# Reordering the first chunk of an attention + max-out kernel: separate softmax for two head pairs, their v parts between weight matmuls, and half of a set of sums moved from POOL to VectorE

## Chip, cores and metric

The kernel runs on one core of a Trainium2 chip. The metric is the device time of one execution in microseconds (us); lower is better. The times quoted are medians of several executions unless said otherwise. Each execution also reports a *span* (first to last instruction) and the *mean granted clock* of TensorE, where 1.0 is full speed. *Throttle* here means a stretch in which that clock is below 1.0, and no more: the profile shows the clock, not what sets it.

In the profile, PE is TensorE (PEld its weight loads), ACT ScalarE, DVE VectorE, POOL GpSimd. `L522` is a source line of the kernel profiled; the change moves line numbers, so the same helper is L522 before and L460 after.

## The reference

```python
k_proj = einsum('ks,bhsd->bhkd', E, k)          # sequence 1024 projected to 64
v_proj = einsum('ks,bhsd->bhkd', F, v)
attn   = softmax(q @ k_proj.T / 8)              # 8 batches, 8 heads, head dim 64
x      = (attn @ v_proj), heads side by side    # 8192 tokens x 512
h      = maximum(maximum(x @ w1, x @ w2), x @ w3)   # 512 -> 768
out    = h @ w_out                              # 768 -> 512
```

## The kernel before

Heads are worked on in four pairs (g = 0 to 3). A pair's output fills one 128-row slice of x, so slice `ct` of the weight matmuls needs only pair `ct`. For one pair, a *k part* or *v part* is the projection of k or v (with E or F), the *score product* is q times projected k, the *value product* is the softmax's exponentials times projected v, and the *scaling* divides that by the exponentials' sum. The token chunk is 512 wide. The order of instructions on each engine is that of the program (`manual_schedule`), and the matmuls' results go to one PSUM tile that the kernel declares as eight banks of 128x512 fp32 and deals out by its own helpers (`bank`, `two`).

The first chunk of the first batch is special. Nothing is loaded yet, so it is arranged around the loads: two pairs are finished first, then matmuls with slices 0 and 1 of w1 and w2 fill TensorE while the other two pairs are prepared. The parts that matter here, with cuts marked:

```python
C0 = (0, SPC)
...                                   # E, F transposed; q and k of pairs 0 and 1
z01 = []
for g in range(2):                    # pairs 0 and 1
    idle(2)                           # matmuls on zeros, to keep TensorE busy
    z01.append(sums(0, g, *C0))
    invert(0, g, *C0, z01[g])         # 1/sum as exp(-ln(sum)) on ACT
    v_pair(g)                         # v projected, copied by DVE
idle(1)
for g in range(2):
    scale_x(0, g, *C0, values(0, g, *C0))
...
def up_first(work):
    ...
    h = six()                         # six banks: w1, slices 0 and 1
    ...                               # copied to s1 (SBUF) by ACT and DVE
    then(0)                           # pairs 2 and 3: q, k, scores, one exp, one sum
    h = six()                         # six banks: w2
    for ct in range(2):
        for jt in jts:
            up_mm(h[jt][0], 1, 0, 0, jt, (ct,))
    then(2)                           # v 2, x 2, v 3, x 3, one after another
    for jt in jts:
        t, ns = bank()
        up_mm(t, 0, 0, 0, jt, (2, 3), first=2)            # w1, slices 2 and 3
        copy("s", s2[:, jt], t, ns)                       # ACT
        nc.gpsimd.tensor_tensor(out=s1[:, jt], in0=s1[:, jt], in1=s2[:, jt], op=ALU.add)
        added = clock["s"] + 1.2
        up_mm(h[jt][0], 1, 0, 0, jt, (2, 3))              # w2, slices 2 and 3
        most(s1[:, jt], *h[jt], s1[:, jt], added)         # DVE maximum
    then(4)
    for jt in jts:                                        # w3, all slices
        t, ns = bank()
        up_mm(t, 2, 0, 0, jt, range(NCT))
        most(hTs[0, 0][:, jt, :], t, ns, s1[:, jt])
        then(5 + jt)                  # second half of the queries, in between
...
up_first({
    0: [lambda: q_duo(1), lambda: k_pair(2), lambda: k_pair(3),
        lambda: attend(1), lambda: idle(3), lambda: sum_duo(1)],
    2: [lambda: v_pair(2), lambda: x_pairs(1, (0,)),
        lambda: v_pair(3), lambda: x_pairs(1, (1,))],
    5: [qp(0, (0, 1), *c1)],          # q transposes of the second half
    6: [qp(0, (2, 3), *c1)],
    7: [sc(0, 0, *c1)],               # its first score product
    8: [sc(0, 1, *c1)],
    10: [za(0, 0, *c1), sc(0, 2, *c1)],
})
```

I call the loop with w1's slices 2 and 3 the *last phase* of w1 and w2, and the score product under key 7 *the first score product of the second half*. That product is a good mile mark: after it both kernels do the same work in the same order.

The softmax here doesn't subtract the row's maximum and nothing guards it: scores larger than these inputs give would overflow.

Of the kernel before, what the change touches and what calls it, by code (L numbers as in the profile page):

```python
# [8 lines left out]
FP32 = mybir.dt.float32  # L9
BF16 = mybir.dt.bfloat16  # L10
AF = mybir.ActivationFunctionType
ALU = mybir.AluOpType
# [3 lines left out]
def kernel(  # L16
# [13 lines left out]
    nc = tc.nc  # L30
# [7 lines left out]
    P = 128  # L38
    HALF = 64
# [34 lines left out]
    def two():  # L74
        n = min(range(0, 8, 2), key=lambda n: max(free[n:n + 2]))
        deal((n, n + 1))
        return psum_t[:, n:n + 2, :], (n, n + 1)
# [6 lines left out]
    def pe(dt, wait=0.0):  # L84
        clock["pe"] = max(clock["pe"], wait) + dt
        return clock["pe"]

    def runs(eng, ready, dt, ns=()):
        if eng in clock:
            clock[eng] = max(clock[eng], ready + 0.06) + dt  # L90
            for n in ns:
                free[n] = clock[eng]
            return clock[eng]
        return ready + dt
# [139 lines left out]
    def sums(b, g, lo, nsi):  # L234
        return pair_mm(b, g, lo, nsi, lambda rows, hp: ones[rows])

    def invert(b, g, lo, nsi, z):
        t, ns, ready = z
        zl = att.tile([P, 2, CHUNK], FP32, name="zl", bufs=1)[:, :, 0:nsi * HALF]
        nc.scalar.activation(out=zl, in_=t, func=AF.Ln)  # L240
        runs("s", ready, 0.17 + nsi * 0.107, ns)
        if nsi == SI:
            zi = att.tile([P, 2, CHUNK], FP32, name="zi", bufs=2)
        else:
            zi = att.tile([P, 2, CHUNK // 2], FP32, name="zi0", bufs=4)
        nc.scalar.activation(out=zi, in_=zl, func=AF.Exp, scale=-1.0)  # L246
        zis[b, g, lo] = zi, runs("s", ready, 0.17 + nsi * 0.107)
# [129 lines left out]
    def idle(n):  # L377

        t, ns = bank()
        for _ in range(n):  # L380
            nc.tensor.matmul(out=t, lhsT=warm[:, 0:P], rhs=warm, start=True, stop=True)  # L381
        free[ns[0]] = pe(n * MM)
# [45 lines left out]
            t.rearrange("a (g si p) -> a g si p", si=SPC, p=P), ns, 0.7,  # L428
        )

    N0 = SPC * HALF

    def sc_duo(u):
        t, ns = two()
        for gg in range(2):
            g = 2 * u + gg
            for c in range(2):
                for hp in range(2):
                    rows = slice(hp * HALF, (hp + 1) * HALF)
                    at = g * SI + c * SPC // 2  # L440
                    nc.tensor.matmul(
                        out=t[c * HALF:(c + 1) * HALF, hp, gg * N0:(gg + 1) * N0],
                        lhsT=kpTs[0][rows, g, :],
                        rhs=qTs[0][rows, at:at + SPC // 2, :],
                        start=True, stop=True,
                    )
        return t, ns, pe(0.5)

    def exp_duo(u, sc):
        t, ns, ready = sc  # L450
        pTs[0, u] = att.tile([P, 2, CHUNK], BF16, name="pT", bufs=4)
        nc.scalar.activation(out=pTs[0, u], in_=t, func=AF.Exp, scale=scale)
        runs("s", ready, 1.0, ns)

    def sum_duo(u):
        t, ns = two()
        for c in range(2):
            rows = slice(c * HALF, (c + 1) * HALF)
            for hp in range(2):
                nc.tensor.matmul(  # L460
                    out=t[hp * HALF:(hp + 1) * HALF, c],
                    lhsT=ones[rows], rhs=pTs[0, u][rows, hp, :],
                    start=True, stop=True,
                )
        ready = pe(0.25)
        zl = att.tile([P, 2, CHUNK], FP32, name="zl", bufs=1)
        nc.scalar.activation(out=zl, in_=t, func=AF.Ln)
        runs("s", ready, 1.0, ns)
        zi = att.tile([P, 2, CHUNK], FP32, name="zi", bufs=2)
        nc.scalar.activation(out=zi, in_=zl, func=AF.Exp, scale=-1.0)  # L470
        zis[0, u] = zi, runs("s", ready, 1.0)

    def x_pairs(u, pairs):

        t, ns = two()
        for i, gg in enumerate(pairs):
            for c in range(2):
                rows = slice(c * HALF, (c + 1) * HALF)
                for hp in range(2):
                    nc.tensor.matmul(  # L480
                        out=t[hp * HALF:(hp + 1) * HALF, c, i * N0:(i + 1) * N0],
                        lhsT=vps[0][rows, 2 * (2 * u + gg) + hp, :],
                        rhs=pTs[0, u][rows, hp, gg * N0:(gg + 1) * N0],
                        start=True, stop=True,
                    )
        ready = pe(0.15 * len(pairs))
        zi, when = zis[0, u]
        for i, gg in enumerate(pairs):
            g = 2 * u + gg
            nc.vector.tensor_tensor(  # L490
                out=xTs[0][:, g, 0:SPC, :].rearrange("a (c s) p -> a c (s p)", c=2),
                in0=t[:, :, i * N0:(i + 1) * N0],
                in1=zi[:, :, gg * N0:(gg + 1) * N0],
                op=ALU.mult,
            )
            runs("v", max(ready, when), 0.69, ns)

    C0 = (0, SPC)
    idle(11)
    turn_ef()  # L500
# [3 lines left out]
    k_pair(1)  # L504
    for g in range(2):
        exps(0, g, *C0, scores(0, g, *C0))
    z01 = []
    for g in range(2):
        idle(2)
        z01.append(sums(0, g, *C0))  # L510
        invert(0, g, *C0, z01[g])
        v_pair(g)
    idle(1)
    for g in range(2):
        scale_x(0, g, *C0, values(0, g, *C0))

    ffn_sb = ctx.enter_context(tc.tile_pool(name="ffn_sb", bufs=2))
    hTs = {}
# [16 lines left out]
    def up_first(work):  # L535


        def then(key):
            run_later()
            for f in work.get(key, []):  # L540
                f()

        s1 = ffn_sb.tile([P, NJT, CHUNK], FP32, name="s1", bufs=1)
        s2 = ffn_sb.tile([P, NJT, CHUNK], FP32, name="s2", bufs=1)
        hTs[0, 0] = ffn_sb.tile([P, NJT, CHUNK], BF16, name="hT")
        jts = range(NJT)

        def six():
            return [(t[:, n], ns[n:n + 1]) for t, ns in (two(), two(), two()) for n in (0, 1)]

        h = six()
        for ct in range(2):
            for jt in jts:
                up_mm(h[jt][0], 0, 0, 0, jt, (ct,), last=1)
                if ct == 1:
                    copy("sv"[jt % 2], s1[:, jt], *h[jt])
        then(0)
        load_k1()
        h = six()
        for ct in range(2):  # L560
            for jt in jts:
                up_mm(h[jt][0], 1, 0, 0, jt, (ct,))
        then(2)
        for jt in jts:
            t, ns = bank()
            up_mm(t, 0, 0, 0, jt, (2, 3), first=2)
            copy("s", s2[:, jt], t, ns)
            nc.gpsimd.tensor_tensor(out=s1[:, jt], in0=s1[:, jt], in1=s2[:, jt], op=ALU.add)
            added = clock["s"] + 1.2
            up_mm(h[jt][0], 1, 0, 0, jt, (2, 3))  # L570
            most(s1[:, jt], *h[jt], s1[:, jt], added)
        then(4)
        for jt in jts:
            t, ns = bank()
            up_mm(t, 2, 0, 0, jt, range(NCT))
            most(hTs[0, 0][:, jt, :], t, ns, s1[:, jt])
            then(5 + jt)
# [132 lines left out]
    for b in range(B):  # L710
        p = plan(b)

        def behind(ch, step):
            for f in p.get((ch, step), []):
                f()

        for ch in range(NCHUNK):
            if (b, ch) == (0, 0):
                c1 = (SPC, SPC)
                def attend(u):  # L720
                    exp_duo(u, sc_duo(u))

                up_first({
                    0: [lambda: q_duo(1), lambda: k_pair(2), lambda: k_pair(3),
                        lambda: attend(1), lambda: idle(3), lambda: sum_duo(1)],
                    2: [lambda: v_pair(2), lambda: x_pairs(1, (0,)),
                        lambda: v_pair(3), lambda: x_pairs(1, (1,))],
                    5: [qp(0, (0, 1), *c1)],
                    6: [qp(0, (2, 3), *c1)],
                    7: [sc(0, 0, *c1)],  # L730
                    8: [sc(0, 1, *c1)],
                    10: [za(0, 0, *c1), sc(0, 2, *c1)],
                })
                run_later()
                behind(0, NJT - 1)
            else:
                for step in range(NJT):
                    up(b, ch, step)
                    behind(ch, step)
            for tt in range(SPC):  # L740
                down(b, ch, tt, "v" if (b, ch) == (0, 0) else "s")
                behind(ch, NJT + tt)
# [30 lines left out]
```

## Time and profile before

| | before |
|---|---|
| time, median of 3 runs | 411.93 us (411.62 to 412.19) |
| span of the profiled execution | 409.9 us |
| PE busy | 394.5 us, 96% |
| DVE, ACT, POOL busy | 200.9, 194.1, 38.6 us |

PE is the bound, so only TensorE's waits, and time at a lower clock, can be won without removing work. The first view is two lines of the page of the kernel before: busy time by engine, and the granted clock in 40 slices of the span (each digit a tenth, 9 is 90% or more; a slice is 10.2 us).

```profile
PE 394.5 (96%) x2452; PEld 180.5 (44%) x2497; DVE 200.9 (49%) x308; ACT 194.1 (47%) x281; POOL 38.6 (9%) x49
...
PEclk9989999999999999999999999999999999999999
```

The third slice of the granted clock is 8: something happens between 20.5 and 30.7 us. The next view is the timeline of that stretch of the kernel before. Its columns are start, duration, engine, source line, operation, output<-input, how many instructions were merged, and in brackets the idle time just ahead with what ended it.

```profile
9.17 0.70 PE L406 MATMUL banks<-efT,k_t 128*64 128x64 bf16 x32
...
21.17 2.76 PE L522 MATMUL banks<-xT,w_sb 128*128 128x512 bf16 x12
...
23.86 0.64 PE L288 MATMUL banks<-v_t,efT 128*64 128x128 bf16 x16
...
24.96 0.30 PE L480 MATMUL banks<-pT,vp 64*64 64x256 bf16 x4 [0.46 <-DVE vp L99]
...
26.13 0.64 PE L288 MATMUL banks<-v_t,efT 128*64 128x128 bf16 x16 [0.87 <-DVE xT L490]
...
27.15 0.30 PE L480 MATMUL banks<-pT,vp 64*64 64x256 bf16 x4 [0.38 <-DVE vp L99]
...
28.25 0.58 PE L522 MATMUL banks<-xT,w_sb 128*128 128x512 bf16 x1 [0.80 <-DVE xT L490]
...
31.67 6.18 POOL L568 TENSOR_TENSOR s<-s,s 128x512 f32<-128x512 f32 x5 [0.45 <-ACT s L99]
...
37.89 0.69 DVE L532 TENSOR_TENSOR s<-banks,s 128x512 f32<-128x512 f32 x1 [0.54 <-PE banks L299]
...
39.09 0.68 DVE L99 COPY qT<-banks 128x1024 bf16<-128x1024 bf16 x1
...
39.83 0.30 PE L207 MATMUL banks<-qT,kpT 64*64 64x256 bf16 x4 [1.00 <-DVE qT L99]
```

Twelve w2 matmuls run to 23.93. Then come v part, copy, value product and scaling (DVE, L490) of pair 2, and the same again for pair 3. The w2 sums hold six of the eight banks, and the two left are handed from one step to the next, so the steps are in series: TensorE works 1.9 us of 4.3. The last phase starts at 28.25. Below it, POOL makes the six w1 additions one after another (6.18 us for five of them); the last maximum on DVE (37.89) waits for the last of these (the view names PE's q transposes, which ended at the same moment, but the earlier maxima name POOL, and so does this one in the profile of e5 below), hence the q copy at 39.09, and TensorE idles 1.00 us until the first score product of the second half at 39.83.

The windows view of the same profile gives busy time of each engine in a stretch (PE, PEld, DVE, ACT, POOL, with the number of instructions in brackets), after it the granted clock (0.75 in the first row), and last two columns on DMA:

```profile
27.00:28.00 1.00, 0.30 (x4) 0.21 (x5) 0.59 (x2) 0.00 (x0) 0.00 (x0) 0.75 1.19 217
28.00:29.00 1.00, 0.58 (x1) 0.25 (x2) 0.20 (x1) 0.00 (x0) 0.00 (x0) 0.50 1.20 192
29.00:30.00 1.00, 0.94 (x3) 0.38 (x3) 0.00 (x0) 0.58 (x1) 0.04 (x1) 0.50 1.44 200
30.00:31.00 1.00, 1.00 (x4) 0.35 (x3) 0.00 (x0) 0.00 (x0) 1.00 (x1) 0.54 1.45 199
```

The clock is 1.00 before and after these four rows. It is halved from the middle of the first until just before 31: (1-0.75)/0.5 + 1 + 1 + (1-0.54)/0.5 = 3.4 us. (In windows of 0.25 us it reads 1.00 in 27.25:27.50, 0.52 in 27.50:27.75, 0.50 until 30.75 and 0.66 in 30.75:31.00.)

### The profile page before, as it was taken

What the parts mean: (1) busy time and instruction counts of PE and PEld (TensorE: products, weight loads), DVE (VectorE), ACT (ScalarE), POOL (GpSimd) and SP (SyncE); (2) the same over time, 40 slices, a digit from 0 to 9 for tenths busy, and PEclk for the clock granted to TensorE, in tenths of its full rate; (3) what the DMA queues carried; (4) which work ended last, traced back from release to release, by engine and by line L of the source; (5) the groups of instructions that cost most, each with busy time, mean ns of one, the idle gap of its engine ahead of it and who ended that gap; (6) DMA issues with size and microseconds to landing.
All of it is one profiled execution on the core that took longest, in us unless ns stands there. A gap on an engine that the chain in (4) does not pass through costs nothing.

```text
span 409.9 us, 6124 instructions
## 1 busy us (share of the span) xinstructions
PE 394.5 (96%) x2452; PEld 180.5 (44%) x2497; DVE 200.9 (49%) x308; ACT 194.1 (47%) x281; POOL 38.6 (9%) x49
## 2 busy tenths in 40 slices
PE   8878999999999999999999999999999999999995
PEld 3434454345444544444544445444544444444443
DVE  2416656464374536636463564525465363525251
ACT  2523627722765266457435555536545556432322
POOL 7328002002000200200020002000000000000000
PEclk9989999999999999999999999999999999999999
DMA  9999937958934994794799109960420202020202
GB/s 169 204 206 196 190 117 112 222 159 125 243 65 114 211 224 139 128 233 83 117 209 224 69 2 244 204 168 0 105 104 1 102 2 102 2 102 0 104 0 103
DMA packets 58492, 52.30 MB, mean 128 GB/s; under 512 B 25952, under 2 KB 54112, under 8 KB 58464
## 3 DMA queue, kind: packets, MB, share of 16 engines
q0 software_dynamic: 28496, 28.31, 43.6%
q1 hardware_dynamic: 29824, 23.46, 18.0%
q8 instruction: 19, 0.31, 0.3%
q10 hardware_dynamic: 144, 0.13, 0.1%
q14 instruction: 9, 0.07, 0.1%
HBM read 57.15 MB, written 16.78 MB: 180 GB/s over the span
## 4 chain that ended last, share of the span: by engine, by line
PE 91%; DVE 3%; ACT 2%; DMA 2%; issue 1%; SPq 0%; DVEq 0%; ACTq 0%
PE banks L522 60%; PE banks L632 19%; PE banks L227 4%; PE banks L288 4%; PE banks L207 2%; DMA ef_f<-in_F_dram 1%; PE banks L299 1%; PE banks L381 1%; DMA out_dram<-o_sb 0%; DVE xT L257 0%; DVE s L99 0%; ACT zl L240 0%; ACT pT L218 0%; DVE xT L490 0%; DVE m L597 0%
## 5 line engine op out<-in xcount | busy, mean ns | idle before, releaser
L522 PE MATMUL banks<-xT,w_sb 128*128 128x512 bf16 x1117 | 255.5, 380 | 3.7 <-DVE xT L490 0.8
L522 PEld LDWEIGHTS <-w_sb 128*128 128x128 bf16 x1152 | 110.0, 98 | 139.5 <-issue 13.5
L597 DVE TENSOR_TENSOR m<-banks,h1s 128x512 f32<-128x512 f32 x90 | 62.1, 690 | 86.3 <-ACT h1s L593 54.7
L593 ACT COPY h1s<-banks 128x512 f32<-128x512 f32 x90 | 52.4, 582 | 92.9 <-PE banks L522 89.7
L632 PE MATMUL banks<-wout_sb,hT 128*128 128x512 bf16 x370 | 84.8, 379 | 0.8 <-issue 0.3
L257 DVE TENSOR_TENSOR xT<-banks,zi 128x1024 bf16<-128x1024 f32 (+1 forms) x34 | 38.3, 1130 | 75.3 <-ACT zi L246 57.7
L532 DVE TENSOR_TENSOR hT<-banks,m 128x512 bf16<-128x512 f32 x90 | 62.3, 692 | 9.7 <-PE banks L522 0.5
L99 ACT COPY o_sb<-banks 128x512 f32<-128x512 f32 (+1 forms) x60 | 34.8, 580 | 53.1 <-PE banks L632 53.0
L632 PEld LDWEIGHTS <-hT 128*128 128x128 bf16 x378 | 36.0, 98 | 45.5 <-issue 3.1
L240 ACT ACTIVATE zl<-banks 128x1024 f32<-128x1024 f32 (+1 forms) x34 | 32.3, 949 | 30.5 <-PE banks L227 30.2
L218 ACT ACTIVATE pT<-banks 128x1024 bf16<-128x1024 f32 (+1 forms) x34 | 32.1, 951 | 7.6 <-PE banks L207 7.6
L246 ACT ACTIVATE zi<-zl 128x1024 f32<-128x1024 f32 (+1 forms) x34 | 33.4, 981 | 1.1
L196 POOL DMA_DIRECT2D q_t<-in_q_dram x7 | 6.2, 882 | 193.9 <-DMA qT<-q_p 70.9
L288 PEld LDWEIGHTS <-efT 128*64 128x64 bf16 x288 | 13.7, 110 | 4.4 <-issue 4.0
L227 PE MATMUL banks<-pT,ones 64*64 64x512 bf16 (+1 forms) x136 | 13.3, 381 | 0.8 <-DVE xT L257 0.3
L207 PE MATMUL banks<-qT,kpT 64*64 64x512 bf16 (+1 forms) x136 | 12.7, 364 | 1.4 <-DVE qT L99 1.0
L99 DVE CAST vp<-banks 64x256 bf16<-64x256 f32 (+1 forms) x18 | 7.1, 397 | 12.5 <-PE banks L288 8.9
L227 PE MATMUL banks<-pT,vp 64*64 64x512 bf16 (+1 forms) x136 | 12.6, 359 | 0.0
L288 PE MATMUL banks<-v_t,efT 128*64 128x256 bf16 (+1 forms) x176 | 9.9, 254 | 0.9 <-DVE xT L490 0.9
L227 PEld LDWEIGHTS <-ones 64*64 64x64 bf16 x136 | 4.0, 103 | 14.9 <-issue 14.9
L99 ACT COPY s<-banks 128x512 f32<-128x512 f32 x9 | 5.1, 588 | 10.5 <-remote 5.9
L381 PE MATMUL banks<-warm 128*128 128x512 bf16 x23 | 8.3, 501 | 1.5 <-DVE warm L165 1.2
(56 smaller groups left out, 118.8 us busy)
## 6 DMA issues: line engine op xcount, KB each, us to landing
out_dram<-o_sb SPq DMA_DIRECT2D x30, 512.0 KB, 3.4
k_t<-in_k_dram POOLq DMA_DIRECT2D x7, 1024.0 KB, 14.1
q_t<-in_q_dram POOLq DMA_DIRECT2D x7, 1024.0 KB, 9.6
v_t<-in_v_dram POOLq DMA_DIRECT2D x7, 1024.0 KB, 18.5
w_sb<-in_moe_w_dram POOLq DMA_DIRECT2D x6, 384.0 KB, 14.4
k_t<-in_k_dram POOLq DMA_DIRECT2D x2, 512.0 KB, 9.4
v_t<-in_v_dram POOLq DMA_DIRECT2D x4, 256.0 KB, 10.7
wout_sb<-in_moe_w_out_dram POOLq DMA_DIRECT2D x1, 768.0 KB, 16.3
```

The costliest lines, as they stand in the source:

```text
L99: done = {"v": nc.vector.tensor_copy, "s": nc.scalar.copy, "g": nc.gpsimd.tensor_copy}[eng](out=o, in_=i)
L218: nc.scalar.activation(out=pTs[b, g, lo], in_=t, func=AF.Exp, scale=scale)
L227: nc.tensor.matmul(out=t[hp * HALF:(hp + 1) * HALF, c, 0:nsi * HALF], lhsT=w(rows, hp), rhs=p[rows, hp, :], start=True, stop=True,)
L240: nc.scalar.activation(out=zl, in_=t, func=AF.Ln)
L246: nc.scalar.activation(out=zi, in_=zl, func=AF.Exp, scale=-1.0)
L257: nc.vector.tensor_tensor(out=xTs[b][:, g, lo:lo + nsi, :].rearrange("a (c s) p -> a c (s p)", c=2), in0=t, in1=zi, op=ALU.mult,)
L288: nc.tensor.matmul(out=t[hh * HALF:(hh + 1) * HALF, 0:width], lhsT=efT[:, si, kv - 1, :], rhs=qkv[b][kv][:, heads[hh], si, :], start=(si = ...
L522: nc.tensor.matmul(out=h, lhsT=w_sb[i][:, ct, jt * P:(jt + 1) * P], rhs=xTs[b][:, ct, ch * SPC:(ch + 1) * SPC, :], start=(ct == first), st ...
L532: nc.vector.tensor_tensor(out=o, in0=h, in1=other, op=ALU.max)
L593: nc.scalar.copy(out=h1s, in_=h[0][0])
L597: nc.vector.tensor_tensor(out=m12, in0=h[1][0], in1=h1s, op=ALU.max)
L632: nc.tensor.matmul(out=o_ps, lhsT=hTs[b, ch][:, jt, tt * P:(tt + 1) * P], rhs=wout_sb[:, jt, :], start=(jt == 0), stop=(jt == NJT - 1),)
```

## The change

The intent: let pair 2 be ready earlier by giving pairs 2 and 3 each their own softmax instead of one shared; put their v parts between w2 matmuls so that TensorE does not stand still while DVE copies and scales; use slice 2 of w2, which needs only pair 2, to cover pair 3; relieve POOL of every second w1 sum. The start is reordered in the same way (pair 0's x before pair 1's v part).

```diff
-    z01 = []
-    for g in range(2):
-        idle(2)
-        z01.append(sums(0, g, *C0))
-        invert(0, g, *C0, z01[g])
-        v_pair(g)
     idle(1)
-    for g in range(2):
-        scale_x(0, g, *C0, values(0, g, *C0))
+    z(0); v_pair(0); z(1)                 # z: sums and their inverse
+    idle(1)
+    x(0); v_pair(1); x(1)                 # x: value product and scaling
 ...
         for ct in range(2):
             for jt in jts:
                 up_mm(h[jt][0], 1, 0, 0, jt, (ct,))
-        then(2)
+            then(1 + ct)
+        for jt in jts:
+            up_mm(h[jt][0], 1, 0, 0, jt, (2,))
+            if jt == 2:
+                then(3)
         for jt in jts:
             t, ns = bank()
             up_mm(t, 0, 0, 0, jt, (2, 3), first=2)
-            copy("s", s2[:, jt], t, ns)
-            nc.gpsimd.tensor_tensor(out=s1[:, jt], in0=s1[:, jt], in1=s2[:, jt], op=ALU.add)
-            ...
+            if jt % 2:
+                copy("s", s2[:, jt], t, ns)
+                nc.gpsimd.tensor_tensor(... op=ALU.add)
+            else:
+                nc.vector.tensor_tensor(out=s1[:, jt], in0=t, in1=s1[:, jt], op=ALU.add)
+            up_mm(h[jt][0], 1, 0, 0, jt, (3,))
+            ...                           # maxima: even jt at once, odd jt two steps later
 ...
-    0: [q_duo(1), k_pair(2), k_pair(3), attend(1), idle(3), sum_duo(1)],
-    2: [v_pair(2), x_pairs(1, (0,)), v_pair(3), x_pairs(1, (1,))],
+    0: [attend],     # q_duo(1), k_pair(2), k_pair(3); exps(2), exps(3); idle(2); z(2), z(3)
+    1: [v_pair(2)],
+    2: [x(2), v_pair(3)],
+    3: [x(3)],
```

(Semicolons and the comments in the diff are mine, to shorten it.)

More of the change, by code (lines that the diff above doesn't have):

```diff
@@ L429, in q_duo @@
         )
-    N0 = SPC * HALF
-    def sc_duo(u):
-        t, ns = two()
-        for gg in range(2):
-            g = 2 * u + gg
-            for c in range(2):
-                for hp in range(2):
-                    rows = slice(hp * HALF, (hp + 1) * HALF)
-                    at = g * SI + c * SPC // 2
-                    nc.tensor.matmul(
-                        out=t[c * HALF:(c + 1) * HALF, hp, gg * N0:(gg + 1) * N0],
-                        lhsT=kpTs[0][rows, g, :],
-                        rhs=qTs[0][rows, at:at + SPC // 2, :],
-                        start=True, stop=True,
-                    )
-        return t, ns, pe(0.5)
@@ L449, in exp_duo @@
-    def exp_duo(u, sc):
-        t, ns, ready = sc
-        pTs[0, u] = att.tile([P, 2, CHUNK], BF16, name="pT", bufs=4)
-        nc.scalar.activation(out=pTs[0, u], in_=t, func=AF.Exp, scale=scale)
-        runs("s", ready, 1.0, ns)
-    def sum_duo(u):
-        t, ns = two()
-        for c in range(2):
-            rows = slice(c * HALF, (c + 1) * HALF)
-            for hp in range(2):
-                nc.tensor.matmul(
-                    out=t[hp * HALF:(hp + 1) * HALF, c],
-                    lhsT=ones[rows], rhs=pTs[0, u][rows, hp, :],
-                    start=True, stop=True,
-                )
-        ready = pe(0.25)
-        zl = att.tile([P, 2, CHUNK], FP32, name="zl", bufs=1)
-        nc.scalar.activation(out=zl, in_=t, func=AF.Ln)
-        runs("s", ready, 1.0, ns)
-        zi = att.tile([P, 2, CHUNK], FP32, name="zi", bufs=2)
-        nc.scalar.activation(out=zi, in_=zl, func=AF.Exp, scale=-1.0)
-        zis[0, u] = zi, runs("s", ready, 1.0)
@@ L473, in x_pairs @@
-    def x_pairs(u, pairs):
-        t, ns = two()
-        for i, gg in enumerate(pairs):
-            for c in range(2):
-                rows = slice(c * HALF, (c + 1) * HALF)
-                for hp in range(2):
-                    nc.tensor.matmul(
-                        out=t[hp * HALF:(hp + 1) * HALF, c, i * N0:(i + 1) * N0],
-                        lhsT=vps[0][rows, 2 * (2 * u + gg) + hp, :],
-                        rhs=pTs[0, u][rows, hp, gg * N0:(gg + 1) * N0],
-                        start=True, stop=True,
-                    )
-        ready = pe(0.15 * len(pairs))
-        zi, when = zis[0, u]
-        for i, gg in enumerate(pairs):
-            g = 2 * u + gg
-            nc.vector.tensor_tensor(
-                out=xTs[0][:, g, 0:SPC, :].rearrange("a (c s) p -> a c (s p)", c=2),
-                in0=t[:, :, i * N0:(i + 1) * N0],
-                in1=zi[:, :, gg * N0:(gg + 1) * N0],
-                op=ALU.mult,
-            )
-            runs("v", max(ready, when), 0.69, ns)
@@ L506, with z, x @@
         exps(0, g, *C0, scores(0, g, *C0))
-    z01 = []
-    for g in range(2):
-        idle(2)
-        z01.append(sums(0, g, *C0))
-        invert(0, g, *C0, z01[g])
-        v_pair(g)
-    idle(1)
-    for g in range(2):
-        scale_x(0, g, *C0, values(0, g, *C0))
+    def z(g):
+        invert(0, g, *C0, sums(0, g, *C0))
+    def x(g):
+        scale_x(0, g, *C0, values(0, g, *C0))
+    idle(1)
+    z(0)
+    v_pair(0)
+    z(1)
+    idle(1)
+    x(0)
+    v_pair(1)
+    x(1)
     ffn_sb = ctx.enter_context(tc.tile_pool(name="ffn_sb", bufs=2))
@@ L566, in up_first @@
             up_mm(t, 0, 0, 0, jt, (2, 3), first=2)
-            copy("s", s2[:, jt], t, ns)
-            nc.gpsimd.tensor_tensor(out=s1[:, jt], in0=s1[:, jt], in1=s2[:, jt], op=ALU.add)
-            added = clock["s"] + 1.2
-            up_mm(h[jt][0], 1, 0, 0, jt, (2, 3))
-            most(s1[:, jt], *h[jt], s1[:, jt], added)
+            if jt % 2:
+                copy("s", s2[:, jt], t, ns)
+                nc.gpsimd.tensor_tensor(
+                    out=s1[:, jt], in0=s1[:, jt], in1=s2[:, jt], op=ALU.add
+                )
+                added = clock["s"] + 1.3
+            else:
+                nc.vector.tensor_tensor(out=s1[:, jt], in0=t, in1=s1[:, jt], op=ALU.add)
+                added = runs("v", clock["pe"], 0.69, ns)
+            up_mm(h[jt][0], 1, 0, 0, jt, (3,))
+            if jt % 2 == 0:
+                most(s1[:, jt], *h[jt], s1[:, jt], added)
+            elif jt > 2:
+                most(s1[:, jt - 2], *h[jt - 2], s1[:, jt - 2], last)
+            if jt % 2:
+                last = added
+        most(s1[:, 5], *h[5], s1[:, 5], last)
         then(4)
@@ L719, with attend @@
                 c1 = (SPC, SPC)
-                def attend(u):
-                    exp_duo(u, sc_duo(u))
+                def attend():
+                    q_duo(1)
+                    k_pair(2)
+                    k_pair(3)
+                    for g in (2, 3):
+                        exps(0, g, *C0, scores(0, g, *C0))
+                    idle(2)
+                    for g in (2, 3):
+                        z(g)
                 up_first({
-                    0: [lambda: q_duo(1), lambda: k_pair(2), lambda: k_pair(3),
-                        lambda: attend(1), lambda: idle(3), lambda: sum_duo(1)],
-                    2: [lambda: v_pair(2), lambda: x_pairs(1, (0,)),
-                        lambda: v_pair(3), lambda: x_pairs(1, (1,))],
+                    0: [attend],
+                    1: [lambda: v_pair(2)],
+                    2: [lambda: x(2), lambda: v_pair(3)],
+                    3: [lambda: x(3)],
                     5: [qp(0, (0, 1), *c1)],
```

## The prediction

> **What bounds the kernel now.** The page has PE busy 394.5 of 409.9 us (96%); the chain of waits is 91% PE. PE's waiting is mostly in the first 50 us; from the timeline (us from the span's start):
>
> - 14.59: first w1 matmul, behind DVE's first xT product (0.69).
> - 21.17: first w2 matmul. Twelve run to 23.93, 0.225 each.
> - 23.93 to 28.25: v part of pair 2, copy, value product, scaling, then pair 3 likewise, in series, since six of eight banks hold w2 sums and the last two are passed on. PE does about 1.9 us of work in 4.3.
> - 28.25 to about 31: matmuls 0.43 us apart. Granted clock 0.50 (28.2-30.2), then 0.64. [...] About 6.5 matmuls lose 0.21 each: 1.4 us.
> - 29.96 to 37.85: six w1 additions on POOL, about 1.24 each. DVE's last maxima wait for them, so the q copy is late (39.09) and PE idles 1.0 us to the score product at 39.83.
>
> **What the change does.** The compared order shows equal PE counts: 4 fewer warm-up matmuls, 4 more sum products. ACT gets two half Exp/Ln/Exp sets (0.55, 0.60, 0.63) for one (1.02, 1.02, 1.06). Three POOL additions with their ACT copies become three DVE additions (0.69 each). w2's third slice (6 matmuls, needing only pair 2) moves ahead of pair 3's product; v parts go between w2 matmuls.
>
> **Worked schedule (estimates from those durations).**
>
> - x of pair 0 no longer waits for pair 1's v part: first w1 matmul about 14.0, twelve done 16.6 (0.6 earlier).
> - Little of this survives: the second half of k lands about 18.3 (PE waits on it now at 17.87-18.31). k parts end 18.95, scores 19.5, sums 20.75. w2 begins about 20.8, 0.4 earlier. Its weights land about 20.35 (POOL's wait).
> - w2 slice 0 to 22.2, v2 22.8, slice 1 24.1, x2 24.4, wait for its scaling (banks) 25.2, v3 25.8, half of slice 2 26.5, x3, rest of slice 2, scaling done 27.5. PE idles about 1 us instead of 2.4 and should stay warm.
> - Last phase starts 27.55, not 28.25, warm, with 18 matmuls left, not 24: saves 0.7 + 1.4 + 1.3. They end about 31.5.
> - Then DVE: 9 operations of 0.69 from 28.05 end about 34.4; POOL's three additions about 33.2. The first q copy ends 35.8, the score product runs about 36.0 instead of 39.83.
>
> So about 3.8 us is saved there. Nothing later should take it back: from bytes at 205 GB/s I estimate w_out landed by 37 (needed 39.7), the next k by 42 (needed 46.7). After that PE does the same work in the same order. 411.93 - 3.85 = about 408.1 us.
>
> **Marks in the profile.** Granted clock 1.00 in 25-32; no PE gap over 1.2 us between 21 and 28; w2 start about 20.8, last phase about 27.5; score product near 36; three POOL additions; later stages shifted 3.5-4.2 us.
>
> **What would make this wrong.** Loads landing later than estimated (second halves of w2/w1, rest of q, near 32-33); the throttle catching PE in 17.2-20.8 or still near 25; DVE's maxima ending after 35, a new wait; bank choices changing further down.
>
> Predicted: 408.1 us, range 406.9 to 409.7; faster by over 2%: 0.02, within 2%: 0.97, slower by over 2%: 0.01.

The 0.21 us for each throttled matmul, and so the 1.4 us, is an estimate that follows from the profile of before: the weight loads of the last phase start 0.43 us apart at clock 0.50 (28.63, 29.06, 29.48, 29.91, 30.34, 30.76), the twelve w2 matmuls at clock 1.00 take 0.225 us each, and 6.5 x (0.43 - 0.225) = 1.3. That TensorE "should stay warm" with shorter stops was the author's assumption. The 205 GB/s is the rate of the DMA in the same profile (204 to 210 GB/s in every window of 5 us from 5 to 40 us); the landing times are estimates from it.

## The result, and the profile after

| | before | after |
|---|---|---|
| median | 412.06 us (411.62 to 412.47, 4 runs) | 408.53 us (408.40 to 409.63, 4 runs) |
| span of the profiled execution | 409.9 us | 407.8 us |
| mean granted clock of the four runs after | | 0.996, 0.999, 1.0, 1.0 |

The ratio is 0.992 (95% interval 0.990 to 0.9941): a gain of 0.8%, clear of noise though well under 2%. A ratio is the mean time of one kernel's runs over that of the other's runs of the same rounds, so it is not quite the ratio of the medians. The prediction was 408.1, range 406.9 to 409.7.

The profile after came from the slowest of the four executions, the one with 409.63 us and clock 0.996. Its page shows why:

```profile
PE 393.8 (97%) x2452; PEld 180.4 (44%) x2497; DVE 202.3 (50%) x311; ACT 192.9 (47%) x281; POOL 34.9 (9%) x46
...
PEclk9899999999999999999999999999999999999999
```

The low digit of the clock has moved to the second slice. The timeline of this execution of the kernel after shows the lines that answer to those above, and one from the start:

```profile
10.51 0.69 PE L406 MATMUL banks<-efT,k_t 128*64 128x64 bf16 x32 [1.61 <-DMA k_t<-in_k_dram]
...
22.78 1.47 PE L460 MATMUL banks<-xT,w_sb 128*128 128x512 bf16 x6
...
27.46 0.64 PE L288 MATMUL banks<-v_t,efT 128*64 128x128 bf16 x16 [0.80 <-DVE xT L257]
...
29.02 5.92 PE L460 MATMUL banks<-xT,w_sb 128*128 128x512 bf16 x25
...
31.91 3.94 POOL L511 TENSOR_TENSOR s<-s,s 128x512 f32<-128x512 f32 x3 [7.42 <-ACT s L99]
...
37.17 0.68 DVE L99 COPY qT<-banks 128x1024 bf16<-128x1024 bf16 x1
...
37.95 0.30 PE L207 MATMUL banks<-qT,kpT 64*64 64x256 bf16 x4
```

TensorE waited 1.61 us for the first half of k, which landed near 10.5 instead of by 9.2. The windows view of this profile finds the halved clock right after:

```profile
12.00:13.00 1.00, 0.72 (x14) 0.71 (x16) 0.00 (x0) 1.00 (x3) 0.72 (x1) 0.75 1.15 205
13.00:14.00 1.00, 1.00 (x17) 0.57 (x13) 0.29 (x1) 0.85 (x2) 0.72 (x1) 0.50 1.29 200
14.00:15.00 1.00, 1.00 (x11) 0.38 (x12) 0.05 (x1) 0.93 (x2) 0.00 (x0) 0.50 1.39 200
15.00:16.00 1.00, 0.82 (x16) 0.58 (x12) 0.78 (x2) 0.30 (x1) 0.71 (x1) 0.55 1.31 220
```

That is again 0.5 + 1 + 1 + 0.9 = 3.4 us at half speed, in another place. So this profile compares an early load and a late throttle (before) with a late load and an early throttle (after). The kernel after was therefore profiled again, unchanged (see the run "after again" below); the execution had clock 1.0 and 408.40 us. Its timeline:

```profile
10.16 0.69 PE L406 MATMUL banks<-efT,k_t 128*64 128x64 bf16 x32 [1.11 <-DMA k_t<-in_k_dram]
...
18.91 0.69 PE L406 MATMUL banks<-efT,k_t 128*64 128x64 bf16 x32 [0.69 <-DMA k_t<-in_k_dram]
...
21.40 1.47 PE L460 MATMUL banks<-xT,w_sb 128*128 128x512 bf16 x6
...
26.18 0.64 PE L288 MATMUL banks<-v_t,efT 128*64 128x128 bf16 x16 [0.80 <-DVE xT L257]
...
27.74 5.92 PE L460 MATMUL banks<-xT,w_sb 128*128 128x512 bf16 x25
...
30.61 3.93 POOL L511 TENSOR_TENSOR s<-s,s 128x512 f32<-128x512 f32 x3 [7.12 <-ACT s L99]
...
33.59 0.64 PE L299 MATMUL banks<-ident,q_t 128*64 128x128 bf16 x16
...
35.88 0.68 DVE L99 COPY qT<-banks 128x1024 bf16<-128x1024 bf16 x1
...
36.66 0.30 PE L207 MATMUL banks<-qT,kpT 64*64 64x256 bf16 x4
```

The longest wait of TensorE between 21 and 28 us is now 0.80 us: the v part of pair 3 waits for the banks that pair 2's value product holds. POOL has three additions. The first score product of the second half stands at 36.66 with no wait ahead. To compare executions whose loads landed at different times, I count it from the first k part (the line of 32 matmuls with `k_t`): 39.83 - 9.17 = 30.66 us before, 36.66 - 10.16 = 26.50 us after.

### The profile page after: what moved, and what is told of

Same layout as the page of the kernel before. It is cut to its first block, busy times and chain, and to the rows that moved or that the text cites. A ratio compares the mean times of both kernels' runs of the same rounds, so it can differ in the third digit from the quotient of the medians. Undisturbed runs are those within 1.5% of the kernel's fastest.

```text
span 407.8 us, 6116 instructions
## 1 busy us (share of the span) xinstructions
PE 393.8 (97%) x2452; PEld 180.4 (44%) x2497; DVE 202.3 (50%) x311; ACT 192.9 (47%) x281; POOL 34.9 (9%) x46
## 4 chain that ended last, share of the span: by engine, by line
PE 91%; DMA 3%; ACT 2%; DVE 2%; issue 1%; POOL 0%; ACTq 0%; DVEq 0%; POOLq 0%
PE banks L460 60%; PE banks L586 19%; PE banks L227 4%; PE banks L288 4%; DMA k_t<-in_k_dram 2%; PE banks L207 2%; PE banks L299 1%; ACT zl L240 1%; DVE xT L257 1%; ACT pT L218 1%; DMA out_dram<-o_sb 0%; DVE s L99 0%; ACT zi L246 0%; DVE m L551 0%; ACT o_sb L99 0%
## 5 line engine op out<-in xcount | busy, mean ns | idle before, releaser
L257 DVE TENSOR_TENSOR xT<-banks,zi 128x1024 bf16<-128x1024 f32 (+1 forms) x36 | 39.8, 1106 | 78.4 <-ACT zi L246 53.7
L240 ACT ACTIVATE zl<-banks 128x1024 f32<-128x1024 f32 (+1 forms) x36 | 33.5, 931 | 30.8 <-PE banks L227 30.6
L218 ACT ACTIVATE pT<-banks 128x1024 bf16<-128x1024 f32 (+1 forms) x36 | 33.2, 931 | 9.7 <-PE banks L207 9.7
L246 ACT ACTIVATE zi<-zl 128x1024 f32<-128x1024 f32 (+1 forms) x36 | 34.6, 962 | 1.1
L99 ACT CAST vp<-banks 64x256 bf16<-64x256 f32 x14 | 5.1, 365 | 7.3 <-PE banks L288 7.1
L99 DVE COPY q_p<-q_t 128x1024 bf16<-128x1024 bf16 x24 | 8.5, 419 | 0.0
```

Source lines behind the costliest of these rows:

```text
L99: done = {"v": nc.vector.tensor_copy, "s": nc.scalar.copy, "g": nc.gpsimd.tensor_copy}[eng](out=o, in_=i)
L218: nc.scalar.activation(out=pTs[b, g, lo], in_=t, func=AF.Exp, scale=scale)
L240: nc.scalar.activation(out=zl, in_=t, func=AF.Ln)
L246: nc.scalar.activation(out=zi, in_=zl, func=AF.Exp, scale=-1.0)
L257: nc.vector.tensor_tensor(out=xTs[b][:, g, lo:lo + nsi, :].rearrange("a (c s) p -> a c (s p)", c=2), in0=t, in1=zi, op=ALU.mult,)
```

## The experiments

Theory: two limits stand in this stretch, TensorE's own stops (with the throttle that I took them to bring) and POOL's chain of additions, and the later one sets the first score product; each part of the change lifts one. Rivals: one part is the whole gain; or the throttle is chance and has nothing to do with the change. All kernels below gave correct results; each was timed in several runs together with the kernel before on the same chip. I call a run *clean* if its mean granted clock was 0.998 or more: one halved stretch of 3.4 us costs (3.4 x 0.5)/410 = 0.004 of the mean clock. The kernel before had three more series of 11 runs with these experiments: 16 of the 33 were clean, mean 411.55 us; the other 17 had a mean of 412.97 us. Twelve of these 17 had a clock of 0.994 to 0.996, about one halved stretch, and a mean of 412.64, 1.1 us above the clean runs; the other five (0.986 to 0.990) lost, by the same sum, more than one such stretch. The clean means on the three chips were 411.57, 411.52 and 411.56, so clean means of different chips can be set side by side. (The clock in the table of all runs is the span's mean; where in the span it fell is seen in profiles only.)

| kernel | mean of the clean runs | clean / all | median of all | ratio to before (95%) |
|---|---|---|---|---|
| before | 411.55 | 16/33 | 411.9 to 412.4 on three chips | |
| e1: only the sums divided | 410.04 | 4/6 | 410.39 | 0.995 (0.9917 to 0.9982) |
| e2: all but the divided sums | 411.00 | 5/6 | 411.03 | 0.9964 (0.9936 to 0.9991) |
| e3, e11: all but the new start | 408.76 and 408.65 | 6/6 and 6/6 | 408.87 and 408.54 | 0.9903 and 0.9917 |
| e4: all but the v parts between | 409.43 | 3/6 | 409.97 | 0.9942 (0.991 to 0.9973) |
| e7: after, again | 408.44 | 5/6 | 408.51 | 0.9915 (0.9895 to 0.9935) |
| e5: before with matmuls on zeros between | 411.41 | 5/6 | 411.42 | 0.9985 (0.9966 to 1.0003) |
| e8: after with four more matmuls on zeros at the start | 408.53 | 6/6 | 408.35 | 0.9914 (0.9893 to 0.9934) |
| e6: after, both v parts early | 408.33 | 6/6 | 408.41 | 0.9906 (0.9888 to 0.9924) |
| e9: the same, q parts later | 407.18 | 4/4 | 407.14 | 0.9881 (0.9861 to 0.990) |
| e10: the same, q load in halves | 407.34 | 4/5 | 407.54 | 0.9888 (0.9868 to 0.9909) |

### Only the sums divided (e1)

To the kernel before, with nothing else changed:

```diff
-            copy("s", s2[:, jt], t, ns)
-            nc.gpsimd.tensor_tensor(... op=ALU.add)
+            if jt % 2:   # ACT and POOL, as before
+            else:        # nc.vector.tensor_tensor(out=s1[:, jt], in0=t, in1=s1[:, jt], op=ALU.add)
```

> The kernel before with only the w1 sums divided between VectorE and POOL. My theory (each part alone gives about a third, together they give all, because after each alone the other limit remains): the throttled stretch near 26-31 us stays, the last phase still starts near 28.2, POOL's chain shrinks from six additions to three, the first score product of the second half moves from 39.8 to about 38.5; time about 410.8 us (1.2 less than before). Rival 1, the division of the sums is the whole gain: 408.5 to 409. Rival 2, the new order of pairs 2 and 3 is the whole gain: 412.

Measured: median 410.39 us, 410.04 in the clean runs, 1.5 us less than the clean runs of before. The timeline of this kernel:

```profile
10.43 0.69 PE L406 MATMUL banks<-efT,k_t 128*64 128x64 bf16 x32 [1.07 <-DMA k_t<-in_k_dram]
...
29.42 6.20 PE L522 MATMUL banks<-xT,w_sb 128*128 128x512 bf16 x27 [0.80 <-DVE xT L490]
...
35.03 1.27 POOL L569 TENSOR_TENSOR s<-s,s 128x512 f32<-128x512 f32 x1 [0.46 <-ACT s L99]
...
38.62 0.30 PE L207 MATMUL banks<-qT,kpT 64*64 64x256 bf16 x4
```

The last phase still starts 19 us after the first k part (29.42 - 10.43; before 28.25 - 9.17 = 19.1). POOL's last addition ends at 36.30, and TensorE reaches the score product without a wait, 28.19 us after the k part. One expectation failed: in this execution the clock did not fall near 26-31 us (1.00 in every window from 24 to 32 us), though TensorE's stops there are the same as in the profile of before (0.46, 0.87, 0.38 and 0.80 us in both). So these stops do not bring the throttle in every execution. Both rivals fall: the divided sums are neither all nor nothing.

### All but the divided sums (e2)

The kernel after, with the six sums back on ACT and POOL (the diff above, the other way).

> The kernel after with all six w1 sums back on ACT and POOL. My theory: last phase starts about 27.5 at full clock, but six POOL additions of 1.24 from about 28.7 end near 36.1, so the score product is near 38.2 and the time about 410.5 us (1.5 to 1.7 less than before, 2 more than after). Rival 1, the division of the sums is the whole gain: 412. Rival 2, the new order is the whole gain: 408.5.

Measured: median 411.03 us, clean 411.00, only 0.55 us under the clean runs of before and less than I expected. The timeline shows what holds it:

```profile
10.14 0.69 PE L406 MATMUL banks<-efT,k_t 128*64 128x64 bf16 x32 [1.40 <-DMA k_t<-in_k_dram]
...
27.45 5.84 PE L460 MATMUL banks<-xT,w_sb 128*128 128x512 bf16 x25
...
29.68 7.41 POOL L510 TENSOR_TENSOR s<-s,s 128x512 f32<-128x512 f32 x6 [6.48 <-ACT s L99]
...
36.64 1.02 PE L460 MATMUL banks<-xT,w_sb 128*128 128x512 bf16 x4 [1.04 <-DVE s L470]
...
39.06 0.30 PE L207 MATMUL banks<-qT,kpT 64*64 64x256 bf16 x4 [1.40 <-DVE qT L99]
```

The last phase comes early and at full clock, but POOL's six additions then take until 37.09. TensorE waits 1.04 us for a bank that a DVE maximum still holds and 1.40 us for the q copy. So TensorE's saving becomes a new wait for POOL. Each part alone gives 1.5 and 0.55 us in clean runs, together 2.1; the whole change gives 411.55 - 408.46 = 3.1 (408.46 is the mean of the eight clean runs of after in both series). The other 1.0 us appears only when both limits are lifted. The mile mark shows the same without the times: counted from the first k part, the score product comes at 29.78 us in the kernel before at full clock (see e5), at 28.19 in e1, at 39.06 - 10.14 = 28.92 in e2 and at 26.50 in after, gains of 1.6, 0.9 and 3.3 us. In e1 TensorE has no wait between the start of the last phase and the score product, so its own order is what is left; in e2 it is POOL.

### All but the new start (e3, and once more e11)

```diff
-    z(0); v_pair(0); z(1); idle(1); x(0); v_pair(1); x(1)
+    (the old loop: idle(2), sums, inverse, v part for each pair; then both x)
```

> The kernel after with the old order of the first part (pairs 0 and 1, before the first w1 matmul). My theory: the first w1 matmul is 0.6 us later, but PE waits for the second half of k anyway, so only 0.2 to 0.4 us of it shows: about 408.8 us. Rival: the earlier first w1 matmul carries through in full and gives 0.6 us of the gain or more: 409.1 or above; second rival: the reordered start is worth nothing: 408.5.

> The kernel after with the old order of the first part, once more on another chip: by ratio to before the first time it was no slower than after (0.9903 against 0.992 and 0.9915). Theory: the new start gives 0.2 to 0.4 us, so 408.8 here against 408.5 for after. Rival: it gives nothing: 408.5 or less.

Measured: 408.87 and 408.54 us, with ratios 0.9903 and 0.9917 against 0.992 and 0.9915 for after. The clean means are 0.2 to 0.3 us above that of after, and the intervals of the ratios are 1.4 to 2.1 us wide. The twelve clean runs together lie 0.25 us above the eight of after, with an interval of about 0.3 either way from their spread: the new start may be worth a few tenths, and the runs do not show that it is worth anything. A likely reason can be read in the profile of after again: up to 18.91 TensorE waits 0.69 us for the second half of k anyway.

### All but the v parts between the w2 matmuls (e4)

```diff
-            then(1 + ct)        # v 2 after slice 0; x 2, v 3 after slice 1
-        for jt in jts: up_mm(..., (2,)) ; x 3 after the third
+        then(2)                 # v 2, x 2, v 3, x 3 after slice 1
 ...
-            up_mm(h[jt][0], 1, 0, 0, jt, (3,))
+            up_mm(h[jt][0], 1, 0, 0, jt, (2, 3))
```

> The kernel after (separate softmax for pairs 2 and 3, divided sums, new start), but the v parts and value products of pairs 2 and 3 once more in one block after the w2 matmuls of slices 0 and 1, and w2's slice 2 at the end with slice 3. My theory: PE has about 2.2 us of waits in 3.9 us there, the granted clock falls to a half near 27-30 us as in the kernel before, and the time is about 410.5 us (2 more than after). Rival: it is the separate softmax (pair 2 ready earlier) that counts and not where the v parts stand: about 409 us, clock 1.0.

Measured: median 409.97 us, clean 409.43, so putting the v parts (and slice 2 of w2) between is worth 1.0 us in clean runs. Its profile had clock 1.00 in 24-34 us, where I expected a half; but three of its six runs were under 0.998. The rival (the separate softmax alone matters, 409 us) is nearer to the clean mean than my 410.5, which assumed the throttle in every run; the mean of all six, three of them throttled, is 410.37. Against e1 (410.04), which has the divided sums alone, the separate softmax and the new start give another 0.6 us; the separate softmax was not run alone.

### After again (e7)

> The kernel after, unchanged, once more: its profile was taken of an execution in which the first half of k landed late (10.5 us) and the clock was halved from 12 to 16 us, and its spread is wanted beside the others. My theory: the block at 24 to 28 us no longer lets the clock fall, so nearly all runs have a mean clock of 0.998 or more, and lie within 408.0 to 409.0 us, while the kernel before has about half of its runs under 0.997 and spreads over 3 us. Rival (the throttle has nothing to do with the change): as many throttled runs as before, and the same spread.

Measured: five of six runs clean, 408.10 to 408.67 us; the sixth 410.05 at 0.995. The kernel before on the same chip had seven of eleven under 0.998.

### Before with matmuls on zeros in the gaps (e5)

```diff
     def x_pairs(u, pairs):
         t, ns = two()
+        for _ in range(2):
+            nc.tensor.matmul(out=t[:, 1], lhsT=warm[:, 0:P], rhs=warm, start=True, stop=True)
```

> The kernel before with two idle matmuls (on a tile of zeros, into the free bank) put after each of the two v parts at 24 to 28 us, in time in which TensorE waits for the copy: no work is added to the chain of waits. If sparse TensorE work in this block is what brings the throttle: fewer throttled runs, the mean about 0.5 us lower (411.5 to 412.0 where before has about 412.4), and the fastest runs the same as before's fastest (411). Rival (throttling falls by chance, whatever the density of the block): same share of throttled runs and same mean.

Measured: median 411.42 us, five of six runs clean, the fastest 411.17 (411.15 for before). The ratio, 0.9985, has an interval that reaches 1.0003, so the mean alone decides nothing. The counts say more. Taking all kernels in which this block is sparse (before, e1, e4), 22 of 45 runs were under 0.998. Of the ten series in which it is filled, by the change or by these idle matmuls, 5 of 55 were. That agrees with the sparse block bringing the throttle, and is hard to square with chance; it is a count over executions, not a picture of each. The two comparisons in which little but the block differs are too small to decide alone: 1 of 6 in e5 against 7 of 11 of before on its chip, and 3 of 6 in e4 against 2 of 10 of after. That POOL's six additions bring it is not seen in e2, which keeps them with the block filled (1 of 6).

This run also shows the kernel before at full clock:

```profile
9.56 0.70 PE L406 MATMUL banks<-efT,k_t 128*64 128x64 bf16 x32 [0.77 <-DMA k_t<-in_k_dram]
...
29.96 7.40 POOL L570 TENSOR_TENSOR s<-s,s 128x512 f32<-128x512 f32 x6 [7.41 <-ACT s L99]
...
37.40 0.69 DVE L534 TENSOR_TENSOR s<-banks,s 128x512 f32<-128x512 f32 x1 [0.54 <-POOL s L570]
...
39.34 0.30 PE L207 MATMUL banks<-qT,kpT 64*64 64x256 bf16 x4 [1.40 <-DVE qT L99]
```

The score product comes 39.34 - 9.56 = 29.78 us after the first k part, against 30.66 in the throttled profile of before. So, between these two profiles, the throttled stretch costs 0.9 us there and not the 1.4 us that its matmuls were estimated to lose. What sets the mile mark in both is the end of POOL's six additions, 37.85 - 9.17 = 28.68 and 37.36 - 9.56 = 27.80 us after the k part, also 0.9 apart; TensorE, less late at full clock, waits longer for it, 1.40 us instead of 1.00.

### After with four more matmuls on zeros at the start (e8)

```diff
-    idle(6)
+    idle(10)
```

> The kernel after with four more idle matmuls before the first k part, where TensorE waits for the load (1.6 us in the profile after). If the throttle in the start (12 to 16 us, seen in one of four runs) comes of this wait: no run with it, a mean as the fastest runs of after (408.3 to 408.6), and no cost as long as k lands after 10.0. If k lands as early as 9.2, as in the profile before, the idle matmuls cost up to 0.7 us.

Measured: 408.35 us, six of six clean, spread 408.00 to 409.53. Against 2 throttled runs in 10 of after, none in 6 cannot be told from chance: inconclusive. Its profile fell on an early k load (POOL's wait for it ended at 9.27), where the extra matmuls held the k part back to 9.82; the expected cost of up to 0.7 us does not show, for that run was the fastest of the six.

### A try for better: both v parts early (e6), and where its gain went (e9, e10)

```diff
         for ct in range(2):
             for jt in jts:
                 up_mm(h[jt][0], 1, 0, 0, jt, (ct,))
-            then(1 + ct)
+                if ct and jt == 2:
+                    then(2)
+            then(1 + 2 * ct)
         for jt in jts:
             up_mm(h[jt][0], 1, 0, 0, jt, (2,))
-            if jt == 2:
-                then(3)
 ...
-    1: [v_pair(2)],            2: [x(2), v_pair(3)],
+    1: [v_pair(2), v_pair(3)], 2: [x(2)],
```

> A try for better: the kernel after, with both v parts (pairs 2 and 3) after w2's slice 0, the value product of pair 2 in the middle of slice 1 and that of pair 3 at its end, so that no v part waits for the banks of a value product (0.80 us of wait in the profile after) and slice 2 covers the scaling of pair 3 (0.25). If TensorE's order alone limits here: 0.8 to 1.0 us less than after, about 407.6. If VectorE's chain of sums and maxima already limits what follows: no gain, 408.5.

Measured: median 408.41 us, no clear gain over after. The timeline shows that TensorE did get ahead, and then what stopped it:

```profile
10.08 0.69 PE L406 MATMUL banks<-efT,k_t 128*64 128x64 bf16 x32 [0.97 <-DMA k_t<-in_k_dram]
...
25.99 0.30 PE L227 MATMUL banks<-pT,vp 64*64 64x256 bf16 x4
...
26.23 6.59 PE L460 MATMUL banks<-xT,w_sb 128*128 128x512 bf16 x28
...
33.91 0.64 PE L299 MATMUL banks<-ident,q_t 128*64 128x128 bf16 x16 [1.09 <-DMA q_t<-in_q_dram]
...
36.98 0.30 PE L207 MATMUL banks<-qT,kpT 64*64 64x256 bf16 x4
```

There is no wait from 24.14 us to the end of the long group at 32.82. Then the q transposes wait 1.09 us for the load of the rest of q. My second branch (DVE's chain) was wrong too: the limit is a DMA. Two ways around it:

```diff
 # e9, added to e6: one w3 group more ahead of the q transposes
-    5: [qp(0, (0, 1), *c1)], 6: [qp(0, (2, 3), *c1)], 7: [sc(0, 0, *c1)], 8: [sc(0, 1, *c1)],
+    6: [qp(0, (0, 1), *c1)], 7: [qp(0, (2, 3), *c1)], 8: [sc(0, 0, *c1)], 9: [sc(0, 1, *c1)],
 # e10, added to e6 instead: the load in two
-    load_q(ALL, slice(SPC, SI))
+    load_q(LO, slice(SPC, SI)); load_q(HI, slice(SPC, SI))
```

> In the try with both v parts early, TensorE waited 1.09 us for the load of the rest of q before its first transposes, and the gain of 1.0 us at the start of the last phase was gone. Here the two q transposes and the two score products that follow each come one w3 group later, so that a w3 group runs while the load lands. If that load is what ate the gain: no such wait, 0.7 to 1.0 us less than that try and than after, about 407.5 to 407.8. Rival: VectorE's chain of sums and maxima limits next, and the time stays at 408.3 to 408.5.

> The other way to the same end: the try with both v parts early, with the load of the rest of q in two halves by heads, so that the first transposes need only the first half (half of 2.5 us earlier, about 32.6). If the load ate the gain: wait under 0.1 us, about 407.5 to 407.8. Rival as for the kernel with later q parts: 408.3 to 408.5. A third outcome, slower than that try, would mean that the smaller loads delay what comes after them.

(The 2.5 us is the author's estimate: this load is 512 KB in the DMA view of before, and moves at about the 205 GB/s seen there.)

Measured: 407.14 and 407.54 us, ratios 0.9881 and 0.9888. All four runs of e9 (406.80 to 407.64) lie below all ten runs of after (408.10 and up; six of them on another chip, the chip of the other four is not on record) and all six of e11 on its own chip (408.12 and up). In e9's profile the wait has shrunk:

```profile
25.67 7.29 PE L460 MATMUL banks<-xT,w_sb 128*128 128x512 bf16 x32
...
33.11 0.64 PE L299 MATMUL banks<-ident,q_t 128*64 128x128 bf16 x16 [0.15 <-DMA q_t<-in_q_dram]
```

0.15 us instead of 1.09. In e10's profile (where this line is L300) it is gone:

```profile
32.58 0.64 PE L300 MATMUL banks<-ident,q_t 128*64 128x128 bf16 x16
```

So the load had eaten the gain: two different ways around it gave the same result. And e9 beats both kernels: 1.2% under before, about 1.3 us under after.

## Why the prediction was right

**The time.** 408.1 predicted, 408.53 measured, inside the range. The predicted saving of 3.85 us compares with 3.5 in the medians, and 3.1 in clean runs. Part of the closeness is luck: the saving was worked out from a throttled profile of before but taken from 411.93, the median of three runs whose clocks are not on record.

**The sum, term by term.**

- *Last phase 0.7 us earlier and six matmuls already done.* Right. Counted from the first k part, the long group of w1 and w2 begins 17.58 us after it (27.74 - 10.16, with three w2 matmuls ahead of the w1 ones) instead of 19.08. On TensorE this was to be 2.0 us (0.7 + 1.3). With the sums divided in both, the q transposes that follow start 35.55 - 10.43 = 25.12 us after the k part in e1 and 33.59 - 10.16 = 23.43 in after, 1.7 us earlier, and the clean times differ by 1.6 (410.04 - 408.46). Of this, 1.0 comes from where the v parts and slice 2 stand (e4), and 0.6 from the separate softmax and the new start.
- *POOL's chain replaced by a DVE chain of about 6.3 us.* Right: from 29.30 (first sum on DVE in the profile of after again) to 35.37 it took 6.07 us. I wrote that DVE then leads; it ends just in time. The q copy ends at 36.56, and TensorE reaches the score product at 36.66 without waiting.
- *Both limits have to go.* The prediction worked this way (last phase first, then DVE), and e1 and e2 bear it out: 1.5 and 0.55 us alone, 3.1 together.
- *1.4 us of throttle removed.* This is the term that was mis-sized. The prediction took the 1.4 us off in full: the throttle in 28-31 us was taken from one profile as if every execution had it. That execution took 411.7 us at a clock of 0.996, no more than clean ones: its first k part came 0.3 to 1.5 us earlier than in the other profiles, which may have hidden the throttle's cost. About half of the runs of before had a mean clock under 0.998 and half did not; and where it strikes, e5 shows that about 0.9 us of it reaches the score product, since POOL's chain hides the rest (in the times, 1.1 us for runs with about one halved stretch). At the mile mark, the throttled profile of before against after again gives 30.66 - 26.50 = 4.16 us, and the one at full clock (e5) 29.78 - 26.50 = 3.28. I predicted 3.85 from the throttled one; without the 0.9 this is about 3.0, and the clean runs show 3.1. The throttle's share of the average gain is (412.28 - 411.55) - (408.73 - 408.46) = 0.46 us, from the means of all and of clean runs of each kernel.
- *New start hardly counts, because of the second half of k.* Right as far as the runs tell; e3 and e11 show 0.2 to 0.3 us, within their noise.

**The marks.** Absolute times were 0.6 to 0.7 us late (w2 at 21.40 for 20.8, score product at 36.66 for 36.0), which goes with later loads: the second half of k held TensorE until 18.91 instead of 18.31, and the profile of before had the earliest first k part of all thirteen profiles, 9.17 us, the others 9.47 to 10.65. Both kernels share that start, so the difference was not hurt. The later stages, to be shifted by 3.5 to 4.2 us, were shifted by 3.3 (spans of 409.9 and 406.6), or 4.3 counted from the k part. The clock stayed at 1.00 in 25-32 in both profiles of after, and no wait was over 1.2 us between 21 and 28. "The rest of q, near 32-33" was named as a risk: it came just in time for after (33.59, no wait) and too late for e6 (33.91).

What stays open: why the first k part begins up to 1.5 us apart (9.17 to 10.65 us) in the thirteen profiles, and whether the early throttle (12-16 us) follows from that wait; e8 did not settle it. It is open, too, where the other throttled runs of before lost their clock: only one throttled run was profiled.

## What to carry to other kernels

When two limits follow each other closely, price each part of a change against the next limit behind it: here the parts gave 1.5 and 0.55 us alone and 3.1 together, and the following try gave nothing until the load behind it was no longer waited for. A single profile is one draw; if its granted clock dips somewhere, look at the clock of several runs before counting that dip as a gain. Where TensorE must wait in short steps on another engine, put matmuls that are needed anyway, and whose inputs are ready, between those steps (here worth 1.0 us in clean runs, e4).
